# A recurrent attention layer and a two-matrix expert on one core: group 2 turned by a transposing DMA, and all steps put in another order

## The chip, the core and the metric

One NeuronCore of a Trainium2 chip. Its engines run side by side, each through its own list of instructions in order, and wait for one another by semaphores: TensorE (PE, matrix products into PSUM), VectorE (DVE), ScalarE (ACT), GpSimd (POOL) and SyncE (SP), whose list holds only DMA issues. The metric is the device time of one execution in microseconds. Three runs of the kernel before gave 175.01, 175.27 and 175.44 us, median 175.27.

## The reference

Two layers follow one another. The first is a linear recurrence for 4 batches, 8 heads, 768 steps and a head width of 48; the second is a product with `w_in`, a smooth gate, and a product with `w_out`.

```python
for t in range(S):
    kt, vt, rt = k[:, :, t], v[:, :, t], r[:, :, t]
    cur = np.einsum('bhd,bhe->bhde', u[None] * kt, vt)
    y[:, :, t] = np.einsum('bhd,bhde->bhe', rt, state + cur)
    state = w[None, :, :, None] * state + np.einsum('bhd,bhe->bhde', kt, vt)
...
x = y.transpose(0, 2, 1, 3).reshape(B * S, H * D)      # 3072 x 384
h = x @ w_in                                           # 384 x 2048
g = np.where(h >= 1, h, np.where(h <= -1, 0, (h + 1) ** 2 / 4))
return g @ w_out                                       # 2048 x 384
```

## The kernel before

**Tiling.** The 768 steps are cut into 6 chunks of 128, the 4 batches into 2 pairs. A *group* g (0 to 11) is one chunk of one pair, so group g has chunk g // 2. A *unit* n (0 to 23) is one batch of a group, n = 2g + j. Inside a chunk the recurrence is computed as matrix products; `states` carry it from chunk to chunk.

**Steps.** The program is a list of small steps, each written as one token in the string `ORDER`. The loop at the end of the kernel walks through it, and each token issues the instructions of one step. A token reads `name.arguments@engine:buffers`; `@A`, `@D` and `@P` choose ACT, DVE or POOL where a step can run on several. The order of the tokens is therefore the order of every engine's list, and nothing is moved afterwards. A `~9` behind a token puts 9 matmuls on zeros ahead of it, and `warm.18` is 18 such matmuls; they compute nothing.

The steps of group g or unit n:

- `load.K.g`, `load.R.g`, `loadV.g` fetch inputs on SP's queue (384 KB each; groups 0 and 1 come in halves `g.0`, `g.1`). `V.g` casts V to bfloat16; the float32 tile that `loadV` fills may be fetched anew only after the cast that reads it.
- `Ks.g`, `Rs.g` scale K and R by powers of the decay (for groups 0 and 1 by the table `tab` in PSUM). `KU.g`, `RKU.g`, `usum.g` and `V2.g` make the diagonal term: K times u, times R, summed over a head, times V.
- `T.n` turns Ks and Rs on PE for groups 0 to 2 and `TT.n` copies the result out; from group 3 on `KRT.K.g` and `KRT.R.g` do it with a transposing DMA on SP's queue.
- `A.n` multiplies the turned tiles, `AT.n` masks the product (DVE in one instruction, or ACT copies and POOL masks).
- `Sp.n`, `Tm.n`, `decay.n`, `sbf.n` move the state on by one chunk. `Y.n` adds state and chunk terms in PSUM, `y.n` adds V2.
- y has to be turned before the second layer. For groups below `X_DMA` this is `X.n` (three transposes on PE) and `xT.n` (a copy out of PSUM by ACT); above it `y` writes into a tile `yy` for both units, and one `xT` of the group is a transposing DMA on SP's queue.
- `w_in.0`, `w_in.1` and `w_out.0` to `w_out.3` load the weights on POOL's queue, in POOL's list.
- `mm1.g.q.j` multiplies a group by quarter q of `w_in` (j = -1 for both units at once), `relu`, `square` (ACT) and `gate` (DVE) make the gated tile, `mm2.g.j.q` multiplies it by a quarter of `w_out`. `o` copies the result out and `out` stores it. The PSUM tiles `h0` to `h2` are shared by T, A and mm1.

**Lines.** `Ks` and `Rs` are L325, `KU` L335, `RKU` L342, `usum` L353 and L355, `V2` L365 and L367, `KRT` L396, `A` L404, `AT` L410 to L419, `Sp` L430, `Tm` L466 to L474, `X` L491, `xT` L501, `mm1` L516, `mm2` L544.

```python
X_DMA = 3
...
if g < X_DMA:
    copy(e, tiles["xT", g][:, j], tiles.pop(("X", n)))
else:
    nc.sync.dma_start_transpose(
        out=tiles["xT", g].rearrange("p u k t -> p (u k) t"), in_=tiles["yy", g].rearrange("p u d -> p (u d)")
    )
```

Of the kernel before, what the change touches and what calls it, by code (L numbers as in the profile page):

```python
# [33 lines left out]
warm.18 load.K.0.0:0 load.R.0.0:0 load.K.0.1 load.R.0.1 load.K.1.0:1 load.R.1.0:1 bcu:0 u_bc@D KU.0.0@P:0 RKU.0.0@P:0  # L34
lw loadV.0.0:0 bcw:1 load.K.1.1 KU.0.1@D loadV.0.1 wcol:0 Wdn_p:0 Ks.0.0@D:0 Wup_p load.R.1.1 Rs.0.0@D:0 wCm
KU.1.0@P:1 loadV.1.0:1 Ks.1.0@D:1 warm.4.h.2 T.0:1 load.K.2.0:2 Wdn RKU.1.0@P:1 Rs.1.0@D:1 Rs.0.1@D V.0.0@A:0
RKU.0.1@P T.2:2~9 TT.0@A:0 usum.0.0@D:0 Ks.1.1@D Ks.0.1@D KU.1.1@P Wup Sp.0:0 TT.2@D:1 A.0:1 V.0.1@A load.R.2.0:2
# [5 lines left out]
relu.0.0:0 X.3:0 Tm.5@D:0 mm1.0.1.0:1 AT.4.0:1 xT.3@A decay.5 square.0.0:0 usum.2.0@D:0 Sp.4:1 mm1.0.1.1 w_out.0 Y.4:0
relu.0.1:1 mm1.1.1.-1:0 gate.0.0:0 square.0.1:1 Tm.4@D:1 mm1.0.2.-1:2 relu.1.1:0 Y.5:1 square.1.1:0 V2.2.0@P:0 w_out.1
y.4:1 gate.0.1:1 w_out.2 X.4:0 w_out.3 mm1.0.3.-1:1 xT.4@A:2 gate.1.1:2 relu.0.2:1 Sp.3:0 y.5:2 mm1.1.0.-1:0
square.0.2:1 Tm.3@D KU.3.0@P:1 decay.4 gate.0.2:3 relu.0.3:0 relu.1.0:1 mm2.0.0.0:1 mm2.0.1.0:0 Ks.3.0@P:0 RKU.3.0@D:1
square.1.0:0 KRT.K.3:0 mm1.1.3.-1:2 mm2.0.1.1 Rs.3.0@P:0 mm2.0.0.1 square.0.3:1 gate.1.0:4 mm2.0.1.2 gate.0.3:5
relu.1.3:1 loadV.3.0:1 mm2.0.0.2 mm1.1.2.-1:0 square.1.3:0 usum.3.0@D:1 mm2.0.0.3 relu.1.2:0 KRT.R.3:0 mm2.0.1.3
o.0.0@D:0 square.1.2:1 mm2.1.0.0:1 o.0.1@D gate.1.3:6 load.K.4.0:1 X.5:0 mm2.1.0.1 load.R.4.0:1 xT.5@A V.3.0@A:3
mm1.2.3.-1:1 gate.1.2:7 sbf.3@A V2.3.0@P:1 Sp.7:0 A.7:2 loadV.4.0:0 relu.2.3:1 Tm.7@D:0 A.6:0 mm2.1.0.2 AT.6.0:2  # L50
sbf.2@A square.2.3:0 Ks.4.0@P:2 sbf.4@A Sp.6:0 mm2.1.0.3 load.K.5.0:2 Tm.6@D:1 mm1.2.0.-1:0 o.1.0@A:1 AT.7.0:3 decay.6
Y.6:0 Y.7:1 relu.2.0:0 KRT.K.4:1 y.6:0 mm1.2.1.-1:2 KU.4.0@P:0 y.7 V.4.0@A:4 gate.2.3:8 xT.6:1 RKU.4.0@P:0
square.2.0:1 mm2.1.1.0:0 Sp.8:1 mm2.1.1.1 load.R.5.0:2 Tm.8@D:1 relu.2.1:1 load.K.6.0:0 mm1.2.2.-1:1 gate.2.0:9
Ks.5.0@P:1 mm2.1.1.2 square.2.1:0 mm2.2.0.0:1 mm2.1.1.3 decay.7 Rs.4.0@P:1 mm1.3.0.-1:0 gate.2.1:0 relu.2.2:0
square.2.2:1 KRT.K.5:0 mm2.2.0.1 o.1.1@D sbf.5@A relu.3.0:1 mm1.3.1.-1:2 gate.2.2:1 out.1 KU.5.0@P:1 square.3.0:0
Rs.5.0@P:2 mm2.2.0.2 relu.3.1:0 gate.3.0:3 mm1.3.2.-1:1 KRT.R.4:1 square.3.1:1 loadV.5.0:1 load.R.6.0:0 usum.4.0@D:0
mm2.2.0.3 mm2.2.1.0:0 KU.6.0@P:0 relu.3.2:1 gate.3.1:5 mm1.3.3.-1:0 square.3.2:0 loadV.6.0:0 gate.3.2:4 mm2.2.1.1
V2.4.0@P:0 sbf.6@A o.2.0@A:1 A.9:2 sbf.7@A relu.3.3:0 A.8:1 AT.9.0:1 mm2.2.1.2 KRT.R.5:0 square.3.3:1 mm2.3.0.0:1
AT.8.0:0 out.0 decay.8 mm2.2.1.3 load.K.7.0:1 mm2.3.0.1 o.2.1@A gate.3.3:2 V.6.0@A:0 V.5.0@A:2 Y.8:0 Ks.6.0@P:0
mm2.3.0.2 y.8:1 Y.9:0 mm2.3.0.3 y.9 RKU.5.0@P:1 A.11:2 xT.8:0 o.3.0@A:0 A.10:1 usum.5.0@D:1 AT.11.0:2 mm2.3.1.0:0  # L60
Sp.10:1 KRT.K.6:1 mm2.3.1.1 Rs.6.0@P:0 RKU.6.0@P:0 Tm.10@D:0 mm2.3.1.2 load.R.7.0:1 Sp.9:1 mm2.3.1.3 Tm.9@D:1
V2.5.0@P:1 mm1.4.0.-1:0 AT.10.0:3 o.3.1@A sbf.8@A decay.9 decay.10 KRT.R.6:1 usum.6.0@D:0 relu.4.0:1 Sp.11:1 Y.10:0
mm1.4.1.-1:2 square.4.0:0 Tm.11@D:1 y.10:0 V2.6.0@P:0 Ks.7.0@P:2 Y.11:1 mm1.4.2.-1:1 loadV.7.0:0 out.2 relu.4.1:0
gate.4.0:7 y.11 A.12:0 xT.10:2 square.4.1:1 AT.12.0:0 mm2.4.0.0:0 Sp.12:1 relu.4.2:1 KU.7.0@P:1 square.4.2:0
gate.4.1:6 load.K.8.0:2 mm1.4.3.-1:0 V.7.0@A:1 KRT.K.7:0 gate.4.2:9 load.R.8.0:2 A.13:2 Rs.7.0@P:1 mm2.4.0.1 out.3
Tm.12@D:0 mm1.5.0.-1:1 AT.13.0:1 RKU.7.0@P:1 relu.4.3:0 square.4.3:1 relu.5.0:1 gate.4.3:0 loadV.8.0:1 square.5.0:0
sbf.9@A decay.12 mm2.4.0.2 Y.12:1 mm1.5.2.-1:2 usum.7.0@D:1 mm2.4.0.3 Ks.8.0@P:1 y.12:1 mm1.5.1.-1:0 gate.5.0:1
o.4.0@A:1 Y.13:1 KRT.R.7:0 relu.5.2:0 V2.7.0@P:1 KRT.K.8:1 Sp.13:0 square.5.2:1 mm1.5.3.-1:1 y.13 Tm.13@D:0 decay.11
relu.5.1:1 xT.12:1 gate.5.2:8 mm2.4.1.0:1 KU.8.0@P:0 Sp.14:0 square.5.1:0 mm2.4.1.1 load.K.9.0:0 Tm.14@D:1 mm2.4.1.2
relu.5.3:0 sbf.10@A gate.5.1:3 mm2.5.0.0:0 Rs.8.0@P:2 A.15:2 square.5.3:1 A.14:0 AT.15.0:3 mm2.4.1.3 mm2.5.0.1  # L70
V.8.0@A:3 KRT.R.8:1 decay.13 RKU.8.0@P:0 AT.14.0:2 mm1.6.0.-1:2 o.4.1@A load.R.9.0:0 gate.5.3:5 Y.14:1 mm2.5.0.2
Ks.9.0@P:0 y.14:0 relu.6.0:1 mm1.6.1.-1:0 square.6.0:0 usum.8.0@D:0 gate.6.0:4 loadV.9.0:0 load.K.10.0:1 mm2.5.0.3
mm2.5.1.0:1 sbf.11@A sbf.12@A A.17:1 relu.6.1:0 o.5.0@D:0 KU.9.0@P:1 A.16:2 mm2.5.1.1 AT.17.0:0 V2.8.0@P:0 decay.14
Rs.9.0@P:0 square.6.1:1 sbf.13@A Y.15:0 mm2.5.1.2 mm1.6.2.-1:1 y.15 V.9.0@A:4 AT.16.0:1 xT.14:0 KRT.K.9:0 Sp.15:0
RKU.9.0@P:1 gate.6.1:2 mm2.5.1.3 load.R.10.0:1 mm1.6.3.-1:2 relu.6.2:1 square.6.2:0 relu.6.3:0 o.5.1@D Tm.15@D:0
mm2.6.0.0:1 gate.6.2:7 out.5 Y.16:0 mm1.7.1.-1:0 decay.15 square.6.3:1 y.16:1 KRT.R.9:0 Ks.10.0@P:2 Sp.17:0 Tm.17@D:1
gate.6.3:6 load.K.11.0:2 mm2.6.0.1 relu.7.1:1 mm1.7.0.-1:1 KU.10.0@P:0 square.7.1:0 sbf.15@A mm2.6.0.2 Sp.16:0
relu.7.0:0 KRT.K.10:1 loadV.10.0:1 gate.7.1:9 mm1.7.2.-1:2 Rs.10.0@P:1 Tm.16@D:0 mm2.6.0.3 square.7.0:1 o.6.0@A:0
sbf.14@A usum.9.0@D:1 Y.17:0 mm1.7.3.-1:0 decay.16 y.17 relu.7.2:1 gate.7.0:0 RKU.10.0@P:0 mm2.6.1.0:1 square.7.2:0
Sp.18:0 KRT.R.10:1 mm2.6.1.1 Tm.18@D:0 sbf.16@A decay.17 A.18:1 gate.7.2:1 out.4 mm2.7.0.0:0 relu.7.3:0 xT.16:2  # L80
KU.11.0@P:1 mm2.6.1.2 square.7.3:1 AT.18.0:2 V2.9.0@P:1 mm2.7.0.1 load.R.11.0:2 loadV.11.0:0 Ks.11.0@P:1 mm2.6.1.3
gate.7.3:3 mm2.7.0.2 A.21:2 sbf.17@A V.10.0@A:2 o.6.1@A A.19:1 AT.21.0:3 A.20:0 mm2.7.0.3 AT.19.0:1 out.6 Y.18:1
o.7.0@A:1 y.18:0 mm1.8.0.-1:2 relu.8.0:1 KRT.K.11:0 AT.20.0:0 Y.19:0 mm1.8.1.-1:1 y.19 mm2.7.1.0:1 square.8.0:0
usum.10.0@D:0 xT.18:1 Sp.19:0 mm2.7.1.1 Tm.19@D:1 relu.8.1:0 mm1.8.2.-1:0 gate.8.0:8 square.8.1:1 mm2.7.1.2 decay.19
V2.10.0@P:0 relu.8.2:1 V.11.0@A:0 gate.8.1:5 Y.20:0 mm2.7.1.3 mm1.8.3.-1:2 decay.18 square.8.2:0 y.20:1 RKU.11.0@P:1
relu.8.3:0 o.7.1@D gate.8.2:4 square.8.3:1 out.7 mm1.9.0.-1:1 Rs.11.0@P:2 mm2.8.0.0:0 relu.9.0:1 gate.8.3:2 Y.21:1
mm2.8.0.1 KRT.R.11:0 usum.11.0@D:1 square.9.0:0 mm1.9.1.-1:0 y.21 xT.20:0 mm1.9.3.-1:2 relu.9.1:0 gate.9.0:7
square.9.1:1 mm2.8.0.2 mm2.8.1.0:1 relu.9.3:1 gate.9.1:6 mm1.9.2.-1:1 square.9.3:0 mm2.8.1.1 mm2.8.0.3 mm2.8.1.2
relu.9.2:0 V2.11.0@P:1 gate.9.3:0 o.8.0@D:0 A.22:0 sbf.19@A square.9.2:1 A.23:2 AT.22.0:2 mm2.8.1.3 mm2.9.0.0:0
AT.23.0:1 mm1.10.3.-1:0 o.8.1@A sbf.18@A Y.22:1 mm2.9.0.1 relu.10.3:1 mm1.10.2.-1:2 y.22:0 gate.9.2:9 Y.23:1  # L90
relu.10.2:0 mm1.10.0.-1:1 y.23 xT.22:2 square.10.2:0 mm2.9.0.2 relu.10.0:0 mm2.9.1.0:1 gate.10.2:1 mm2.9.0.3
square.10.0:1 mm2.9.1.1 mm1.10.1.-1:2 square.10.3:0 out.8 gate.10.0:3 mm2.9.1.2 gate.10.3:8 relu.10.1:0 mm1.11.0.-1:1
# [535 lines left out]
```

## Time and profile before

| what | value |
|---|---|
| median of three runs | 175.27 us |
| the profiled execution: its time, its span | 175.03 us, 173.3 us |
| first matmul of the second layer (mm1.0.0) | 21.46 us after the span's start |
| end of the last matmul | 169.8 us |
| TensorE clock granted | 1.00 in every slice |
| packets of the SP queue | 103888, 25.27 MB, 75.2% of 16 DMA engines' span |

A row of the profile gives a start and a duration in us, the engine, the line, the operation, the tiles it writes and reads, and in brackets the idle time of the engine before it with what ended it. Line numbers in the profile of before are those of the listing above. The span is shorter than the time of the execution by 1.7 us, which lie outside the program's instructions.

### The profile page before, as it was taken

How to read it: one execution, taken by the hardware profiler on the slowest of the kernel's cores; microseconds unless marked ns; L12 is line 12 of the kernel's file. 1: busy time of each engine (PE TensorE's matmuls, PEld its weight loads, DVE VectorE, ACT ScalarE, POOL GpSimd, SP SyncE). 2: the span in 40 equal slices, each digit the busy share in tenths (PEclk: the TensorE clock that was granted, in tenths of full speed). 3: DMA queues.
4: the chain of work that ended last, by engine and by line, in shares of the span. 5: the costliest groups of instructions: out<-in, count | busy, mean ns of one | idle time of the engine just before them, and what ended most of it. 6: DMA issues, size and time to landing. Idle time of an engine off the chain costs nothing.

```text
span 173.3 us, 4141 instructions
## 1 busy us (share of the span) xinstructions
PE 163.5 (94%) x1674; PEld 123.7 (71%) x1674; DVE 134.8 (78%) x168; ACT 134.9 (78%) x194; POOL 118.1 (68%) x96
## 2 busy tenths in 40 slices
...
GB/s 110 224 223 198 223 185 232 201 173 206 240 175 200 246 159 255 154 186 238 183 235 182 210 213 155 232 229 253 229 77 95 106 2 4 128 8 95 0 91 91
...
## 3 DMA queue, kind: packets, MB, share of 16 engines
q1 hardware_dynamic: 103888, 25.27, 75.2%
q0 software_dynamic: 2912, 3.15, 11.3%
...
## 4 chain that ended last, share of the span: by engine, by line
PE 71%; DMA 10%; DVE 9%; ACT 5%; issue 2%; POOL 1%; SPq 1%; DVEq 0%; POOLq 0%
PE hp L516 33%; PE op L544 30%; DMA VF<-in_v_dram 5%; DVE AT L419 3%; DMA xT<-yy 3%; PE A L404 3%; DVE RKU L342 2%; DMA K<-in_k_dram 2%; DVE gt L534 2%; PE Y L444 2%; PE Y L439 2%; PE Sp L430 1%; ACT V L210 1%; ACT RKU L353 1%; POOL V L367 1%
## 5 line engine op out<-in xcount | busy, mean ns | idle before, releaser
L516 PE MATMUL hp<-xT,w_in_sb 128*128 128x256 bf16 (+1 forms) x600 | 70.8, 268 | 2.7 <-DVE gt L534 1.0
L544 PE MATMUL op<-w_out_sb,gt 128*128 128x384 bf16 x384 | 71.7, 326 | 0.0
L534 DVE SCALAR_TENSOR_TENSOR gt<-sq,hp 128x1024 bf16<-128x1024 f32 x48 | 57.9, 1216 | 14.6 <-ACT sq L529 14.3
L516 PEld LDWEIGHTS <-w_in_sb 128*128 128x128 bf16 x600 | 55.8, 98 | 12.8 <-issue 2.9
L524 ACT ACTIVATE pt<-hp 128x1024 f32<-128x1024 f32 x48 | 48.6, 1017 | 13.5 <-PE hp L516 13.3
L529 ACT ACTIVATE sq<-pt 128x1024 f32<-128x1024 f32 x48 | 50.4, 1057 | 3.0 <-DVE gt L534 1.8
L544 PEld LDWEIGHTS <-gt 128*128 128x128 bf16 x384 | 35.6, 98 | 19.7 <-issue 0.2
L419 DVE TENSOR_TENSOR AT<-A,umask 128x1024 bf16<-128x1024 f32 x22 | 26.5, 1218 | 1.8 <-PE A L404 1.5
L367 POOL TENSOR_TENSOR V<-V,diag 128x768 f32<-128x768 bf16 (+1 forms) x12 | 16.5, 1375 | 9.1 <-ACT V L210 7.1
L335 POOL TENSOR_TENSOR KU<-K,u_bc 128x768 f32<-128x768 f32 (+1 forms) x13 | 21.3, 1640 | 1.9 <-DVE u_bc L210 1.8
L342 POOL TENSOR_TENSOR RKU<-R,KU 128x768 f32<-128x768 f32 (+1 forms) x13 | 20.7, 1595 | 0.3
L325 POOL TENSOR_TENSOR Ks<-Wdn,K 128x768 bf16<-128x768 f32 x10 | 18.3, 1828 | 2.1 <-PE Y L444 1.7
L479 POOL TENSOR_TENSOR state<-Tm,wCm 128x384 f32<-128x384 f32 x16 | 16.1, 1008 | 5.1 <-DVE Tm L466 5.1
L325 POOL TENSOR_TENSOR Rs<-Wup,R 128x768 bf16<-128x768 f32 x10 | 18.3, 1830 | 0.0
L458 DVE TENSOR_TENSOR yy<-Y,V 128x384 bf16<-128x384 f32 x18 | 9.9, 553 | 5.0 <-PE Y L444 3.5
L210 ACT CAST V<-VF 128x768 bf16<-128x768 f32 (+1 forms) x14 | 10.2, 736 | 2.7 <-DMA VF<-in_v_dram 2.7
L466 DVE TENSOR_TENSOR Tm<-Sp,state 128x384 f32<-128x384 f32 x16 | 8.9, 553 | 4.3 <-PE Sp L430 3.4
L444 PE MATMUL Y<-V,AT 128*128 128x48 bf16 x192 | 11.2, 184 | 1.1 <-POOL AT L414 0.7
L210 ACT COPY oo<-op 128x384 f32<-128x384 f32 x13 | 6.2, 475 | 7.6 <-PE op L544 7.5
L444 PEld LDWEIGHTS <-AT 128*128 128x128 bf16 x192 | 9.5, 96 | 2.7 <-POOL AT L414 1.0
L355 DVE TENSOR_REDUCE diag<-RKU 128x16 f32<-128x768 f32 (+1 forms) x13 | 11.0, 850 | 0.0
L210 ACT CAST state_bf<-state 128x384 bf16<-128x384 f32 x20 | 10.0, 504 | 0.0
...
## 6 DMA issues: line engine op xcount, KB each, us to landing
out_dram<-oo SPq DMA_DIRECT2D x11, 384.0 KB, 3.3
K<-in_k_dram SPq DMA_DIRECT2D x10, 384.0 KB, 4.6
R<-in_r_dram SPq DMA_DIRECT2D x10, 384.0 KB, 4.1
VF<-in_v_dram SPq DMA_DIRECT2D x10, 384.0 KB, 5.7
...
w_out_sb<-in_moe_w_out_dram POOLq DMA_DIRECT2D x4, 384.0 KB, 7.4
...
```

The source lines that it names most:

```text
L210: nc.scalar.copy(out, in_) if e == "A" else engines[e].tensor_copy(out, in_)
L325: engines[e].tensor_mul(of_unit(dst, j0, j1)[:, :, :, :D], rep(tab, j1 - j0), of_unit(tiles[what, g], j0, j1))
L335: engines[e].tensor_mul(of_unit(tiles["KU", g], j0, j1), of_unit(tiles["K", g], j0, j1), rep(u_bc, j1 - j0))
L342: engines[e].tensor_mul(of_unit(tiles["RKU", g], j0, j1), of_unit(tiles["R", g], j0, j1), of_unit(tiles["KU", g], j0, j1))
L367: engines[e].tensor_mul(tiles["V2", g][:, hs, :], tiles["V", g][:, hs, :], tiles["diag", g][:, hs].unsqueeze(2).to_broadcast([P, hs.stop - ...
L419: nc.vector.tensor_mul(t.rearrange("p i n t -> p (i n) t"), tiles.pop(("A", n)).rearrange("p i n t -> p (i n) t"), umask.unsqueeze(1).to_b ...
L444: nc.tensor.matmul(t[:, 2 * p + i, :], tiles["AT", n][:, i, p, :], tiles["V", g][:, j * H + 2 * p + i, :], start=(c == 0), stop=True, skip ...
L516: nc.tensor.matmul(hp[:, f, cols], w_in_sb[:, i, n0 : n0 + P], tiles["xT", g][:, units, i, :], start=(i == 0), stop=(i == nK - 1), skip_gr ...
L524: nc.scalar.activation(tiles["pt", g, q], tiles["hp", g, q], AF.Relu, bias=0.5, scale=0.5)
L529: nc.scalar.activation(tiles["sq", g, q], tiles.pop(("pt", g, q)), AF.Square, bias=0.0)
L534: nc.vector.scalar_tensor_tensor(out=gt, in0=tiles.pop(("sq", g, q)), scalar=1.0, in1=tiles.pop(("hp", g, q)), op0=ALU.min, op1=ALU.max)
L544: nc.tensor.matmul(tiles["op", g, j], tiles["gt", g, q][:, f, j * P : (j + 1) * P], w_out_sb[:, n, :], start=(n == 0), stop=(n == nF - 1),)
```

## The change

`X_DMA` goes from 3 to 2: y of group 2 (units 4 and 5) goes into `yy`, and one transposing DMA on SP's queue takes the place of `X.4`, `X.5` (six PE transposes) and the two copies `xT.4`, `xT.5` on ACT. The string `ORDER` is another one from end to end. Within it some steps change engine: `RKU.3` goes from DVE to POOL; `KU.0.0`, `RKU.0.0` go from POOL to DVE and `KU.0.1` from DVE to POOL; `TT.0` goes from ACT to DVE; `Tm.0` and `Tm.2` go from DVE to ACT, where each is eight small multiplies; `usum.1.0` from ACT to DVE; the four half steps V2 of groups 0 and 1 trade places between ACT and POOL; and of the copies `o` seven go from DVE to ACT (0.1, 1.1, 5.1, 8.0, 10.0, 10.1, 11.0) and two from ACT to DVE (4.0, 7.0). Matmuls on zeros are 54 in place of 68. The constants `W_OUT = 4` and `FUSE = ()` and the branch on `FUSE` are new; with these values they issue the same instructions as before.

```diff
 TABLES = 2
 W_IN = 2
+W_OUT = 4
+FUSE = ()
 NSPLIT = 2
 SPLIT = 2
 T_DMA = 3
 T_TAG = "h"
-X_DMA = 3
+X_DMA = 2
...
-    n = slice(i * FG, (i + 1) * FG)
+    n = slice(i * nF // W_OUT, (i + 1) * nF // W_OUT)
...
-    nc.vector.tensor_add(t, flat(tiles.pop(("Y", n))), flat(tiles["V2", g][:, j * H : (j + 1) * H, :]))
+    Yn = tiles.pop(("Y", n))
+    if g in FUSE:
...
+    else:
+        nc.vector.tensor_add(t, flat(Yn), flat(tiles["V2", g][:, j * H : (j + 1) * H, :]))
...
-T.4:0 TT.5@D:0 Y.1:0 w_in.1 load.K.3.0:0 xT.0@A:1 sbf.1@A usum.1.1@D A.5:1 mm1.0.0.0:2 KU.2.0@P:0 y.1:2 TT.4@D:1
+V2.0.1@P A.4:0~2 TT.5@D:3 load.K.3.0:0 V2.1.0@P:1 Tm.1@D y.2:1 w_in.1 Y.3:0 A.5:1 sbf.0@A V2.1.1@A Y.1:1 sbf.1@A
```

The prediction speaks of three places in the order. The first is ACT's list from the cast of V of unit 2 to the first relu. Before (L353 is usum, the rows V_340 and V_333 are V2, L210 is any copy or cast):

```order
L210 CAST V<-VF 128x384
L353 ACTIVATE RKU,diag<-RKU 128x48 x8
L365 ACTIVATE V_340<-V,diag 128x48 x8
L210 CAST state_bf<-state 128x384
L410 CAST AT<-A 128x1024
L365 ACTIVATE V_333<-V,diag 128x48 x8
L210 COPY xT<-X 128x384 x2
L210 CAST state_bf<-state 128x384
L210 CAST V<-VF 128x384
L210 COPY xT<-X 128x384
L210 CAST V<-VF 128x768
L524 ACTIVATE pt<-hp 128x1024
```

And in the changed kernel, over the same stretch (L482 is Tm, once for unit 0 and once for unit 2; line numbers are about 10 higher at the end of the file):

```order
L212 CAST V<-VF 128x384
L482 ACTIVATE state<-Sp,wc_col 48x48 x16
L412 CAST AT<-A 128x1024
L212 COPY xT<-X 128x384
L212 CAST V<-VF 128x384 x2
L212 CAST state_bf<-state 128x384
L367 ACTIVATE V_454<-V,diag 128x48 x8
L212 CAST state_bf<-state 128x384
L212 COPY xT<-X 128x384
L212 CAST V<-VF 128x768
L212 COPY xT<-X 128x384 x2
L534 ACTIVATE pt<-hp 128x1024
```

The casts of the second halves of V (the row x2) now stand behind Tm and AT.1; before, that of unit 0 stood ahead of everything shown. Two copies xT stand behind the cast of V of group 2.

The second place is POOL's list from the second half of `w_in` to the scaling of group 3. Before:

```order
L288 DMA w_in_sb<-in_moe_w_in_dram 128x3x1024
L335 TENSOR_TENSOR KU<-K,u_bc 128x768
L367 TENSOR_TENSOR V_340<-V,diag 128x384
L342 TENSOR_TENSOR RKU<-R,KU 128x768
L479 TENSOR_TENSOR state<-Tm,wCm 128x384
L292 DMA w_out_sb<-in_moe_w_out_dram 128x4x384
L367 TENSOR_TENSOR V_670<-V,diag 128x768
L292 DMA w_out_sb<-in_moe_w_out_dram 128x4x384 x3
L335 TENSOR_TENSOR KU<-K,u_bc 128x768
L479 TENSOR_TENSOR state<-Tm,wCm 128x384
L325 TENSOR_TENSOR Ks<-Wdn,K 128x16x48
L325 TENSOR_TENSOR Rs<-Wup,R 128x16x48
```

In the changed kernel:

```order
L290 DMA w_in_sb<-in_moe_w_in_dram 128x3x1024
L294 DMA w_out_sb<-in_moe_w_out_dram 128x4x384
L337 TENSOR_TENSOR KU<-K,u_bc 128x768
L344 TENSOR_TENSOR RKU<-R,KU 128x768
L369 TENSOR_TENSOR V_618<-V,diag 128x768
L294 DMA w_out_sb<-in_moe_w_out_dram 128x4x384
L489 TENSOR_TENSOR state<-Tm,wCm 128x384
L294 DMA w_out_sb<-in_moe_w_out_dram 128x4x384 x2
L337 TENSOR_TENSOR KU<-K,u_bc 128x768
L327 TENSOR_TENSOR Ks<-Wdn,K 128x16x48
L344 TENSOR_TENSOR RKU<-R,KU 128x768
L327 TENSOR_TENSOR Rs<-Wup,R 128x16x48
```

`w_out.0` is issued right behind `w_in.1`; `w_out.1` stands behind V2 of group 2, and RKU of group 3 has come in between Ks and Rs of group 3.

The third place is SP's list around the new transposing DMA. Before, from the load of V of group 2:

```order
L302 DMA VF<-in_v_dram 128x16x48
L302 DMA K<-in_k_dram 128x16x48
L302 DMA R<-in_r_dram 128x16x48
L396 DMA_TRANSPOSE KT<-Ks 128x8x128
L302 DMA VF<-in_v_dram 128x16x48
L396 DMA_TRANSPOSE RT<-Rs 128x8x128
L302 DMA K<-in_k_dram 128x16x48
```

In the changed kernel:

```order
L304 DMA VF<-in_v_dram 128x16x48
L304 DMA K<-in_k_dram 128x16x48
L304 DMA R<-in_r_dram 128x16x48
L398 DMA_TRANSPOSE KT<-Ks 128x8x128
L511 DMA_TRANSPOSE xT<-yy 128x6x128
L304 DMA K<-in_k_dram 128x16x48
L398 DMA_TRANSPOSE RT<-Rs 128x8x128
L304 DMA VF<-in_v_dram 128x16x48
```

The new xT stands directly behind the KT of group 3, and V of group 3 is fetched behind RT of that group.

More of the change, by code (lines that the diff above doesn't have):

```diff
@@ L28 @@
 T_TAG = "h"
-X_DMA = 3
+X_DMA = 2
 ORDER = """
[L34 to L37, printed above, removed]
@@ L43 @@
[L43 to L47, printed above, removed]
@@ L48 @@
[L48 to L92, printed above, removed]
@@ L93 @@
[L93 to L97 removed]
+warm.18 load.K.0.0:0 bcu:0 lw load.R.0.0:0 u_bc@D KU.0.0@D:0 RKU.0.0@D:0 usum.0.0@D:0 loadV.0.0:0 load.K.0.1
```

76 lines of the change are left out of this document (67 added, 9 removed).

## The prediction

> **What bounds the kernel now.** First the page's busy times and its chain of waits, then the table by stretches.
>
> ```profile
> PE 163.5 (94%) x1674; PEld 123.7 (71%) x1674; DVE 134.8 (78%) x168; ACT 134.9 (78%) x194; POOL 118.1 (68%) x96
> PE 71%; DMA 10%; DVE 9%; ACT 5%; issue 2%; POOL 1%; SPq 1%; DVEq 0%; POOLq 0%
> 45.00:70.00 25.00, 24.93 (x254) 18.31 (x253) 19.44 (x23) 21.61 (x28) 24.92 (x16) 1.00 1.20 210
> 70.00:90.00 20.00, 18.63 (x219) 14.62 (x219) 16.55 (x20) 14.37 (x18) 19.44 (x15) 1.00 1.02 197
> 90.00:170.00 80.00, 79.78 (x764) 59.12 (x762) 59.48 (x66) 63.22 (x75) 39.12 (x26) 1.00 0.61 128
> ```
>
> The columns behind a stretch are its length and the busy time of PE, weight loads, DVE, ACT and POOL. PE is the bound: 71% of the chain. From 90 us on it lacks 0.22 us of 80, so a new order has nothing to win there and can only lose. From 45 to 90 us it is idle for 0.07 + 1.37 = 1.44 us, and POOL is busy for 44.4 of 45. What is left is the start, where the chain leaves PE. PE's "busy" there contains matmuls on zeros, so I read the chain in order of time instead (start, duration):
>
> ```profile
> 9.69 0.40 ACT V L210
> 10.09 0.91 ACT TT L210
> ...
> 11.88 0.91 ACT AT L410
> 12.80 0.43 ACT V L210
> ...
> 15.10 8.50 DMA VF<-in_v_dram
> ...
> 23.63 0.84 ACT V L210
> ...
> 26.56 0.87 DVE diag L355
> ...
> 27.58 1.48 POOL V L367
> ...
> 34.32 4.15 DVE RKU L342
> ...
> 46.91 0.17 PE Sp L430 x4
> ...
> 49.05 0.04 PE Y L439
> ...
> 49.79 1.31 PE hp L516 x12
> ...
> 57.14 0.65 PE op L544 x4
> ...
> 70.02 4.57 DMA xT<-yy
> ```
>
> ACT's list paces the start; then the load of V of group 2, issued at 15.1, holds ACT until 23.6. PE's prices come from here too: a quarter of mm1 1.31 us, of mm2 0.65, one Sp 0.17, and two Y from 49.05 to 49.79, so 0.37 for one. Single steps, from the timeline (start, duration, in brackets the idle time ahead and what ended it):
>
> ```profile
> 14.94 0.84 POOL L367 TENSOR_TENSOR V<-V,diag 128x384 f32<-128x384 bf16 x1
> 14.94 1.90 ACT L365 ACTIVATE V<-V,diag 128x48 f32<-128x48 bf16 x8
> 19.86 0.84 ACT L210 COPY xT<-X 128x384 bf16<-128x384 bf16 x2
> 20.31 0.80 POOL L288 DMA_DIRECT2D w_in_sb<-in_moe_w_in_dram  x1
> 24.36 1.02 ACT L524 ACTIVATE pt<-hp 128x1024 f32<-128x1024 f32 x1
> 27.34 1.21 DVE L534 SCALAR_TENSOR_TENSOR gt<-sq,hp 128x1024 bf16<-128x1024 f32 x1
> 28.61 1.47 PE L516 MATMUL hp<-xT,w_in_sb 128*128 128x256 bf16 x12 [0.17 <-DVE gt L534]
> 35.80 1.84 POOL L325 TENSOR_TENSOR Rs<-Wup,R 128x768 bf16<-128x768 f32 x1
> 39.69 1.06 ACT L529 ACTIVATE sq<-pt 128x1024 f32<-128x1024 f32 x1 [1.77 <-DVE gt L534]
> 45.54 0.62 PE L404 MATMUL A<-RT,KT 48*128 48x128 bf16 x16
> ```
>
> The 28.61 row is mm1.0.2, the first step that needs a PSUM tile back from a gate and the second half of `w_in`; the 45.54 row is A of group 3. Between these two I compare the orders. Landing times of DMAs from their issue, of the tiles VF and w_in_sb (both up to 50 us) and xT, and two lines of the DMA view:
>
> ```profile
> DMA to landing us min/median/max: 3.8/5.0/9.6
> ...
> DMA to landing us min/median/max: 8.0/8.3/8.5
> ...
> DMA to landing us min/median/max: 2.7/2.8/4.6
> ...
> w_out_sb<-in_moe_w_out_dram POOLq DMA_DIRECT2D x4, 384.0 KB, 7.4
> ...
> RT<-Rs SPq DMA_TRANSPOSE x9, 4.6
> ```
>
> **The change, part by part.** *PE's own work.* X.4 and X.5 go: 0.34 us, three transposes priced like the four matmuls of Sp. The work between mm1.0.2 and A of group 3 is counted from each order. Before: six quarters of mm1, ten of mm2, one Y, two X, two Sp: 7.86 + 6.50 + 0.37 + 0.34 + 0.34 = 15.41 us. That took 45.54 - 28.61 = 16.93, so 1.5 us were stalls. Now: the same mm1 and mm2 and one Sp, 14.53 us; Y.5 stands ahead of the stretch, X.4 and X.5 are gone, and one Sp comes behind it (+0.17).
>
> *DVE's new first steps.* KU.0.0, RKU.0.0 and usum.0.0 now stand ahead of Ks.0.0, with which ACT's second table, T.0 and A.0 begin.
>
> ```profile
> 5.68 0.99 POOL L335 TENSOR_TENSOR KU<-K,u_bc 128x384 f32<-128x384 f32 x1 [1.83 <-DVE u_bc L210]
> 5.74 1.35 DVE L335 TENSOR_TENSOR KU<-K,u_bc 128x384 f32<-128x384 f32 x1
> ...
> 7.01 0.55 DVE L325 TENSOR_TENSOR Ks<-tab,K 128x384 bf16<-128x384 f32 x1
> ...
> 34.03 1.85 POOL L325 TENSOR_TENSOR Ks<-Wdn,K 128x768 bf16<-128x768 f32 x1
> ```
>
> DVE's KU ended at 7.09, 0.42 us behind POOL's. RKU of group 3, started at 34.32, ended at 38.47, 0.83 us behind POOL's Rs (35.80 + 1.84): it stood through two POOL products. So half a group of such a product costs DVE 0.42 alone. POOL's KU.0.1 has to wait for its load, now one place later, so I let DVE go first: Ks.0.0 starts at 5.74 + 0.42 + 0.42 + 0.55 (usum, priced like Ks) = 7.1 to 7.2, 0.2 late. If KU.0.1 gets in first, RKU.0.0 waits 1.0 more. [...]
>
> *ACT up to the first relu.* Ahead of the copy AT.0 the list loses V.0.0, V.0.1 (0.40 each) and TT.0 (0.91) and gains V2.0.0 (1.90): +0.2. With DVE's 0.2, AT.0 starts at 12.3 instead of 11.88. Behind it come V.1.0 0.43, Tm.0 and Tm.2, AT.1 0.91, xT.0 0.42 and V.0.1 0.40. A Tm on ACT is eight small multiplies and has no row; the nearest is the ACT row of eight at 1.90, its lower bound a single instruction, 0.40, its upper 2.1 if PSUM is slower. I take 1.90 twice. V.0.1 ends at 12.3 + 0.91 + 0.43 + 3.80 + 0.91 + 0.42 + 0.40 = 19.2. Only then may SP fetch V of group 2 into the tile that V.0.1 read: 4.1 us later than at 15.1, with K and R of group 3 queued behind it on SP. Between the median 5.0 and the maximum 9.6 I take 5.7, a little over the median since both halves of `w_in` are under way: it lands at 24.9. The cast (0.84) and two copies xT (0.84) now stand ahead of relu.0.0: 26.6 against 24.36. Relu, square and gate take 1.02 + 1.06 + 1.21 and some 0.2 between them. **mm1.0.2 starts at 30.1 instead of 28.61: +1.5.** `w_in.1` comes close but does not decide: AT.0's mask on POOL is 0.4 late and one more half of V2 (0.84) stands ahead of it, so it is issued at 20.31 + 1.2 = 21.5 and lands at 29.8. `w_in.0`, behind AT.0's mask now, is covered by ACT's delay.
>
> *From there to A of group 3.* ACT gives a gate every 2.08 us. mm1.1.2 needs the second at 32.2, some 0.6 after PE could start it. `w_out.1` stands on POOL behind KU.2, RKU.2 (1.84 each, like Rs), and V2.2 (1.48), which waits for usum.2 (0.87): from `w_out.0`'s end at 23.1 that is 29.2, landing at 36.6 by 7.4, where PE wants it at 36.1. With a further 0.2 at a gate the stalls are 1.3 to 1.4, as before: RKU.3, which kept DVE from its gates for 4.15 us and ACT idle for 1.77, does so no longer, and the late start gives that back. Ks.3 ends on POOL at 36.4, with decay and two `w_out` issues ahead of it; KT leaves SP then and the new xT behind it at 37.8. It lands 2.7 to 4.6 later, at 42.4 at worst; mm1.2.3 stands at 43.4, so **the new DMA is hidden** by 1 us, and what it comes later than that it costs. RKU.3 moves Rs.3 on POOL from 37.64 to 40.1; RT, 4.6 behind, lands at 44.7, under A at 46.0. V of group 3 is fetched only behind RT, near 41.4: landing (5.0), cast (0.84), V2 (1.48), y (0.55) and transpose (4.6) end at 53.9, and mm1 of group 3 starts 9.5 us of PE work behind A, at 55.5: covered by 1.6 us. Together: +1.5 - (15.41 - 14.53) - 0.1 + 0.17 = **+0.7**. Bounds: V of group 2 lands in 3.8, so `w_in.1` holds mm1.0.2 at 29.8, and no stall is left: 0.7 - 0.3 - 1.4 = -1.0. V lands in 8.5, as that load did before: 0.7 + 2.8 = +3.5.
>
> *From 45 to 90 us.* PE's one wait for a transposing DMA was that of group 4:
>
> ```profile
> PE hp L516 <- DMA xT<-yy: 1.0, 1, 1.0
> ```
>
> Between that group's last Y and its first mm1 stand 4.15 us of PE work before and 3.67 now (counted like the work above): with a landing of 4.57 again the wait grows by 0.5. Group 8 has 3.99 (8.17 before): a wait of 0 to 1.1. The shortest stretch from an mm1 to its mm2 falls from 3.81 to 3.22 us, under the 3.5 of relu, square and gate. If xT lands in 2.8, no such wait is left. I take +0.4, with bounds of -1.4 (all idle time gone) and +1.6. The copies `o` that change engine hide under the next mm2.
>
> **Sum.** The profiled execution took 175.03 us (its span of 173.3 and 1.7 around it), 0.24 below the median of 175.27. 175.03 + 0.7 + 0.4 = **176.1 us**.
>
> **Rivals.** *Faster (0.28).* The loads are less crowded: while SP waits for V.0.1, K and R of group 2 drain, V of group 2 lands in 3.8 and `w_out.1`, issued apart from the others, in 5. Nothing stalls up to A of group 3, -1.0, and xT of group 4 at 2.8 takes its 1.0 too: 173.0; with one of the two, 174.0. It decides if relu.0.0 starts before 25. For it: a queue that stands still leaves room. Against: the POOL chain to `w_out.1` is made of its own durations.
>
> *Much slower (0.17).* V of group 2 shares the DMA engines with `w_in` and takes 8.5 as before: relu.0.0 at 29.4, +2.8, giving 178.9. It decides from a landing past 27. For it: that very load took 8.50 in the chain. Against: then three loads were in the queue ahead of it.
>
> *No change (0.13).* The new DMA is hidden, and what the start loses (0.7) shorter transposes give back from 45 to 90 us: 175.0.
>
> **How the numbers follow.** The forecast, a small loss, has 0.42, its own range 175.3 to 177.3. About 0.3% (0.5 us) is what a measurement of this kernel can tell from no change. Faster is the first rival and a sliver of the forecast: 0.30. Same is the third: 0.13. Slower is the rest: 0.57. The range for 8 in 10 reaches from 173.7, past half of the first rival, to 179.0, past the second's figure.
>
> **What would show it.** Right: the cast of V of group 2 ends past 25, relu.0.0 is near 26.6, mm1.0.2 near 30.1, A of group 3 near 46.0; PE does not wait for xT of group 2 and waits 1 to 1.5 us for that of group 4. Wrong: that cast before 24.5, a Tm on ACT far from 1.9 us, RKU.0.0 on DVE over 0.6, or new PE waits past 90 us, which I have not priced.

## The result, and the profile after

| | before | after |
|---|---|---|
| median of three runs | 175.27 us | 178.36 us (178.07 to 178.37) |
| ratio after to before | | 1.0173, 95% interval 1.0147 to 1.0198 |
| the profiled execution: its time, its span | 175.03 us, 173.3 us | 178.07 us, 176.4 us |

The changed kernel is slower by 3.1 us. Some executions of one and the same kernel take longer than its others (one of b_x2 178.84 us, its nine others 174.61 to 176.35); the ratios of this document leave out those over 1.5% above the fastest. The forecast of 176.1 was added up from the profiled execution of before, so it is to be held against the profiled 178.07: 2.0 us have to be found. First the same views as before: the busy times and the chain of the changed kernel's page.

```profile
PE 164.8 (93%) x1654; PEld 125.4 (71%) x1654; DVE 128.8 (73%) x163; ACT 139.0 (79%) x196; POOL 119.1 (68%) x96
PE 55%; DMA 17%; ACT 9%; POOL 8%; issue 4%; DVE 3%; SPq 1%; ACTq 0%; POOLq 0%
```

PE's share of the chain fell from 71% to 55%, and DMA's rose from 10% to 17%: more of the end is set by transfers. DVE lost 6 us of work and ACT gained 4. The table by stretches of the changed kernel (length; busy time of PE, weight loads, DVE, ACT, POOL; granted clock; DMA share; GB/s) tells where:

```profile
15.00:25.00 10.00, 6.97 (x112) 6.17 (x109) 6.97 (x11) 9.70 (x30) 7.90 (x8) 0.83 0.88 154
45.00:70.00 25.00, 24.58 (x259) 18.33 (x258) 20.66 (x23) 21.13 (x28) 23.18 (x15) 1.00 1.11 216
70.00:90.00 20.00, 19.70 (x218) 14.95 (x216) 16.75 (x20) 16.95 (x22) 18.98 (x14) 1.00 1.10 205
100.00:110.00 10.00, 8.73 (x92) 6.31 (x91) 7.95 (x11) 6.12 (x8) 7.47 (x6) 1.00 1.02 205
120.00:130.00 10.00, 9.78 (x94) 7.30 (x91) 8.26 (x9) 9.37 (x13) 10.00 (x8) 1.00 1.08 205
```

And two of the same stretches in the kernel before:

```profile
15.00:25.00 10.00, 8.15 (x147) 6.77 (x148) 7.96 (x14) 8.38 (x26) 9.98 (x8) 1.00 1.12 195
...
100.00:110.00 10.00, 10.00 (x113) 7.65 (x112) 8.59 (x12) 8.57 (x10) 10.00 (x7) 1.00 0.94 207
```

PE lost 1.2 us of busy time between 15 and 25, and 1.3 between 100 and 110, where it had not been idle at all. From 45 to 90 it is now idle for 0.42 + 0.30 = 0.72 us, against 1.44 before.

Because the orders differ, one start time against another says little. So I add to the start of a group's first mm1 the PE work that still stands behind it in that order, at the prediction's prices. This is where PE would end if it never waited again; the difference after minus before is the loss so far.

| first mm1 of group | started before | started after | loss so far |
|---|---|---|---|
| 0 | 21.46 | 25.31 | +3.0 |
| 2 | 43.97 | 44.57 | +1.9 |
| 6 | 95.86 | 95.63 | +1.1 |
| 7 | 107.60 | 109.33 | +2.6 |
| 9 | 131.32 | 134.43 | +3.1 |
| 11 | 153.32 | 155.77 | +3.1 |

So the start lost 1.9, the middle gave 0.8 back, and 2.0 went late: 1.5 at one place near 104 us and 0.5 between groups 7 and 9.

**The start.** The timeline of the changed kernel (start, duration, in brackets the idle time ahead and what ended it):

```profile
14.98 4.93 ACT L482 ACTIVATE state<-Sp,wc_col 48x48 f32<-48x48 f32 x16 [1.16 <-PE Sp L432]
19.96 0.48 PE L501 MATMUL X<-ident,y 128*128 128x128 bf16 x3 [2.12 <-ACT state L482]
21.02 1.09 POOL L416 TENSOR_SCALAR_AFFINE_SELECT AT<-AT 128x1024 bf16<-128x1024 bf16 x1 [2.08 <-ACT AT L412]
21.35 0.93 ACT L212 CAST V<-VF 128x384 bf16<-128x384 f32 x2
21.89 0.37 SPq L304 DMA_DIRECT2D VF<-in_v_dram  x1
22.08 1.61 POOL L369 TENSOR_TENSOR V<-V,diag 128x384 f32<-128x384 bf16 x2
23.64 0.80 POOL L290 DMA_DIRECT2D w_in_sb<-in_moe_w_in_dram  x1
...
26.87 0.83 ACT L212 CAST V<-VF 128x768 bf16<-128x768 f32 x1
28.35 1.05 ACT L534 ACTIVATE pt<-hp 128x1024 f32<-128x1024 f32 x1
32.43 1.48 PE L526 MATMUL hp<-xT,w_in_sb 128*128 128x256 bf16 x12 [0.56 <-DMA w_in_sb<-in_moe_w_in_dram]
47.33 0.62 PE L406 MATMUL A<-RT,KT 48*128 48x128 bf16 x16
```

The two Tm on ACT took 4.93 us, and ACT first waited 1.16 us for the Sp that they read. Three engines stand behind them. PE waited 2.12 us, because X.0 writes into the PSUM tile from which Tm reads. POOL waited 2.08 us for AT.1, and `w_in.1` stands behind that mask and two halves of V2: issued at 23.64, it ends the wait of mm1.0.2 at 32.43. SP could fetch V of group 2 only after V.0.1, the first of the two casts at 21.35: that load was issued at 21.89, and its cast ran at 26.87.

**Near 104 us.** SP's queue and ACT's list, both of the changed kernel:

```profile
96.56 1.22 SPq L583 DMA_DIRECT2D out_dram<-oo  x1
97.84 0.46 SPq L304 DMA_DIRECT2D VF<-in_v_dram  x1
...
103.45 0.83 ACT L212 CAST V<-VF 128x768 bf16<-128x768 f32 x1 [2.30 <-DMA VF<-in_v_dram]
104.33 0.33 PE L432 MATMUL Sp<-V,Ks 128*128 128x96 bf16 x4 [1.27 <-ACT V L212]
```

The load of V of group 8 is issued at 97.84, lands 5.6 us later, is cast, and Sp of group 8 has waited 1.27 us for it. In the new order 4.8 us of PE work lie between that load's place and this Sp; before there were 23.7. From group 3 on, the other groups of the new order have 8.5 to 12.2 up to their first Sp (group 3 has 5.8 up to a Y, which reads its V first). The shortest such stretch that the order of before has from group 3 on is that of group 4, 5.8, and PE did not wait there.

### The profile page after: what moved, and what is told of

It is laid out like the page before. It is cut to its first block, busy times and chain, and to the rows that moved or that the text cites. A ratio compares the mean times of both kernels' runs of the same rounds, so it can differ in the third digit from the quotient of the medians.

```text
span 176.4 us, 4091 instructions
## 1 busy us (share of the span) xinstructions
PE 164.8 (93%) x1654; PEld 125.4 (71%) x1654; DVE 128.8 (73%) x163; ACT 139.0 (79%) x196; POOL 119.1 (68%) x96
## 4 chain that ended last, share of the span: by engine, by line
PE 55%; DMA 17%; ACT 9%; POOL 8%; issue 4%; DVE 3%; SPq 1%; ACTq 0%; POOLq 0%
PE hp L526 24%; PE op L554 24%; DMA VF<-in_v_dram 5%; DMA w_in_sb<-in_moe_w_in_dram 5%; DMA xT<-yy 4%; ACT sq L539 3%; DMA R<-in_r_dram 2%; ACT pt L534 2%; POOL Rs L327 2%; PE Y L441 1%; PE Y L446 1%; PE A L406 1%; POOL AT L416 1%; ACT state_bf L212 1%; DMA u_row<-in_u_dram 1%
## 5 line engine op out<-in xcount | busy, mean ns | idle before, releaser
L344 POOL TENSOR_TENSOR RKU<-R,KU 128x768 f32<-128x768 f32 (+1 forms) x13 | 21.3, 1639 | 0.4
L468 DVE TENSOR_TENSOR yy<-Y,V 128x384 bf16<-128x384 f32 x20 | 10.9, 554 | 5.3 <-POOL V L369 2.5
L357 DVE TENSOR_REDUCE diag<-RKU 128x16 f32<-128x768 f32 (+1 forms) x14 | 11.5, 830 | 0.5 <-POOL RKU L344 0.5
L212 ACT COPY oo<-op 128x384 f32<-128x384 f32 x17 | 7.9, 472 | 1.3 <-PE op L554 1.0
```

Of the source, the lines that this page charges most:

```text
L212: nc.scalar.copy(out, in_) if e == "A" else engines[e].tensor_copy(out, in_)
L344: engines[e].tensor_mul(of_unit(tiles["RKU", g], j0, j1), of_unit(tiles["R", g], j0, j1), of_unit(tiles["KU", g], j0, j1))
```

## The experiments

Twelve kernels were run. Each diff is by tokens of `ORDER` against the kernel that is named.

| run | kernel and edit | ratio to before | 95% interval |
|---|---|---|---|
| b_x2 | before, group 2's y by DMA alone | 1.0013 | 0.9987 to 1.0039 |
| b_tm_act | before, Tm.0 and Tm.2 on ACT | 1.0301 | 1.0267 to 1.0334 |
| a_tm_dve | changed, Tm.0 and Tm.2 on DVE | 1.0139 | 1.0096 to 1.0181 |
| a_win1 | changed, `w_in.1` earlier | 1.0357 | 1.0285 to 1.0428 |
| a_tm_wo | a_tm_dve, `w_out.1` earlier | 1.0107 | 1.0068 to 1.0146 |
| a_out4 | changed, store of group 4 behind load of V of group 8 | 1.0215 | 1.0181 to 1.0248 |
| a_v8 | changed, load of V of group 8 earlier | 1.0167 | 1.0127 to 1.0207 |
| a_oo | changed, third tile `oo` for o.5.0 | 1.0224 | 1.0195 to 1.0253 |
| a_v8_oo | changed, a_v8 and a_oo | 1.0214 | 1.0187 to 1.0241 |
| a_tm_v8_oo | changed, a_tm_dve, a_v8 and a_oo | 1.0148 | 1.0088 to 1.0208 |
| a_tm_wo_v8 | a_tm_wo and a_v8 | 1.0206 | 1.0141 to 1.0272 |
| a_tm_late | a_tm_v8_oo, xT of group 7 ahead of two loads | 1.0235 | 1.0163 to 1.0307 |

The changed kernel itself is at 1.0173. 0.01 of a ratio is 1.75 us.

### The parts alone, in the order of before

**b_x2.** The headline of the change without the new order:

```diff
-X_DMA = 3
+X_DMA = 2
-X.4:0 X.5:0 xT.4@A:2 xT.5@A
-y.5:2
+y.5 xT.4:2
```

> The kernel before with X_DMA = 2 alone: X.4, X.5 and their two ACT copies go, one transposing DMA is issued on SP behind y.5, the order is else that of before. Theory (the new DMA is hidden; the loss is all in the order): 0.2 to 0.6 us faster than before, 174.7 to 175.1. Rival (the transposing DMA in the crowded early queue delays KT or the loads of group 3): 175.8 to 177.

No change can be told: by the interval it lies between 0.2 us faster and 0.7 us slower, so the theory's gain is not there, and of the rival's loss its lower end at most. In the order of before, the transposing DMA in place of six transposes is not where the time went; that leaves the new order. The new order with `X_DMA` = 3 was not run; in the changed kernel PE waits neither for this DMA nor for the RT of group 3 behind it.

**b_tm_act.** The one move on which the start seemed to hang, put into the order of before:

```diff
-Tm.0@D
+Tm.0@A
-Tm.2@D
+Tm.2@A
```

> The kernel before with Tm.0 and Tm.2 on ACT, nothing else. Theory S: ACT's list gets 4.9 us longer ahead of the first relu, which starts 2 to 4 us behind 24.36; 1 to 2.5 us slower, 176.3 to 177.8. Rival (ACT has room at the start, as its waits for V of group 2 show): 175.1 to 175.7.

This alone costs 5.2 us, more than the whole change and twice the most that its theory gave. Its timeline:

```profile
13.04 2.45 ACT L472 ACTIVATE state<-Sp,wc_col 48x48 f32<-48x48 f32 x8
16.08 0.33 PE L430 MATMUL Sp<-V,Ks 128*128 128x96 bf16 x4 [2.09 <-ACT V L210]
20.06 2.46 ACT L472 ACTIVATE state<-Sp,wc_col 48x48 f32<-48x48 f32 x8
22.56 0.48 PE L444 MATMUL Y<-V,AT 128*128 128x48 bf16 x8 [3.82 <-ACT state L472]
```

One Tm takes 2.45 us, and PE waits 2.09 us behind the first (for the cast that follows it on ACT) and 3.82 behind the second. In this order usum and V2 stand on ACT between the two, which the new order has put elsewhere; so the 5.2 us are the price of the move in a list not made for it, and not a term of the change's sum.

**a_tm_dve.** The reverse, in the changed kernel:

```diff
-Tm.0@A
+Tm.0@D
-Tm.2@A
+Tm.2@D
```

> The changed kernel with Tm.0 and Tm.2 back on DVE, nothing else. Theory S (the two Tm on ACT, 4.93 us there, hold AT.1 and V.0.1 and through them the second half of w_in and V of group 2): AT.1's mask on POOL starts near 19.0 instead of 21.02, w_in.1 is issued near 21.6 instead of 23.64, mm1.0.2 starts near 30.3 instead of 32.43, and the time falls by 1.0 to 1.5 us, to 176.9 to 177.4. Rival (the place of w_in.1 on POOL, behind two halves of V2, or the colder TensorE clock sets the start): no more than 0.4 us, 178.0 to 178.4.

Rows of its timeline:

```profile
21.64 0.80 POOL L290 DMA_DIRECT2D w_in_sb<-in_moe_w_in_dram  x1
26.54 1.05 ACT L534 ACTIVATE pt<-hp 128x1024 f32<-128x1024 f32 x1
30.07 0.80 POOL L294 DMA_DIRECT2D w_out_sb<-in_moe_w_out_dram  x1
37.37 0.81 PE L554 MATMUL op<-w_out_sb,gt 128*128 128x384 bf16 x4 [1.27 <-DMA w_out_sb<-in_moe_w_out_dram]
```

The waits behind Tm are gone: first mm1 at 23.50 in place of 25.31, the first relu 1.81 us earlier. But PE then waits 1.27 us for `w_out.1`, and the first mm1 of group 2 starts at 44.31, 0.26 earlier than in the changed kernel. The ratio is lower by 0.0034 or 0.6 us, inside both intervals, less than the theory's 1.0 and more than the rival's 0.4. Of 1.8 us gained at 25 us, most is given back by 44.

### Two more repairs of the start

**a_win1** issues `w_in.1` ahead of POOL's first scaling of group 2; **a_tm_wo** is a_tm_dve with `w_out.1` right behind `w_out.0`.

```diff
-w_in.1
-Ks.2.0@P:2
+w_in.1 Ks.2.0@P:2
```

```diff
-w_out.1
-w_out.0
+w_out.0 w_out.1
```

> The changed kernel with the second half of w_in issued on POOL ahead of Ks of group 2 instead of behind two halves of V2, Tm still on ACT. Theory S (Tm on ACT is the cause, w_in.1 only the last link): PE's wait of 0.56 us for w_in.1 goes, the first matmul of the second layer stays near 25.3, and the time falls by 0 to 0.5 us, to 177.9 to 178.4. Rival (the place of w_in.1 is the cause of the late start): 1 us or more, 177.4 or less.

> The changed kernel with both Tm on DVE and, on POOL, w_out.1 directly behind w_out.0 instead of behind V2 of group 2. Theory (with Tm gone from ACT the next thing that ends last at the start is w_out.1, for which PE waited 1.27 us at 37.37): that wait goes and the time falls by a further 0.8 to 1.3 us against Tm on DVE alone (177.75), to 176.4 to 177.0. Rival (w_out.1 earlier takes the bandwidth of K and R of group 3, and KT, RT or xT come late instead): 177.5 to 178.2.

`w_in.1` early is 3 us worse than the changed kernel, which neither the theory nor the rival had. PE's longest waits in it:

```profile
PE Y L446 <- ACT V L212: 2.2, 1, 2.2
PE X L501 <- ACT state L482: 2.1, 1, 2.1
...
PE A L406 <- DMA RT<-Rs: 1.2, 2, 1.0
```

The wait for `w_in` is gone, but PE waits 2.2 us for the cast of the second half of V of group 1, whose load, issued at 13.31, landed some 12.3 us later (Y started at 26.16, behind a cast of 0.51), against 5.8 in the changed kernel, and A waits 1.0 us for an RT. With `w_in.1` earlier the loads of V come late in its place, so this run does not tell which of the two held the start. a_tm_wo has the lowest ratio of all edits of the changed kernel: 1.0107, 1.2 us under the changed kernel with intervals that just touch, but not to be told from a_tm_dve. Its ratio rests on two executions (177.48 and 177.78 us), and the profiled one took 180.57, so I read no amounts from it; PE waits there for `w_out` still, and, as the rival said, for RT of group 3.

### The place near 104 us

**a_out4** and **a_v8** try the load of V of group 8 from two sides: the store ahead of it goes behind it, or the load itself goes up, behind the load of K of group 9.

```diff
-out.4
-loadV.8.0:0
+loadV.8.0:0 out.4
```

```diff
-load.K.9.0:0
+load.K.9.0:0 loadV.8.0:0
-loadV.8.0:0
```

> The changed kernel with the store of group 4 moved on SP behind the load of V of group 8, nothing else. Theory L (the store waits for the copy of op on ACT until 96.6 and holds the load of V of group 8 behind it, for which PE waits 1.27 us at 104.33): that load is issued near 96.1 instead of 97.84, PE's wait goes, and the time falls by 1.0 to 1.6 us, to 176.8 to 177.4. Rival (the load is late because the DMA engines are crowded, or the wait only moves): 178.0 to 178.5.

> The changed kernel with the load of V of group 8 moved forward on SP, from behind the store of group 4 to directly behind the load of K of group 9, nothing else. Theory L2 (a lead too short: 4.8 us of PE work lie between that load and the Sp that needs it, 23.7 before, and landing 5.5 and cast 0.84 need 6.3): it is issued near 92.9 instead of 97.84, PE's wait of 1.27 us at 104.33 goes, and the time falls by 1.0 to 1.6 us, to 176.8 to 177.4. Rival (the DMA engines are so crowded there that another load or RT comes late in its place, as with the store moved): 178.0 to 178.6.

In a_out4, without the store ahead of it, the load was issued 0.57 us earlier, at 97.27, and Sp's wait grew from 1.27 to 1.78 us. In a_v8, with the load at 92.75, the cast ran at 100.61 without waiting, and Sp waited all the same. From the timeline of a_v8:

```profile
97.52 1.20 SPq L583 DMA_DIRECT2D out_dram<-oo  x1
...
103.41 0.56 DVE L212 COPY oo<-op 128x384 f32<-128x384 f32 x1 [1.54 <-DMA out_dram<-oo]
...
104.12 0.33 PE L432 MATMUL Sp<-V,Ks 128*128 128x96 bf16 x4 [1.29 <-DVE oo L212]
```

A second cause had been ending at the same moment. o.5.0 copies into the tile `oo` that the store of group 4 still reads, and Sp needs the PSUM tile that o.5.0 empties. The rows of a_out4 fit this: the store went from 96.56 to 98.61 there, the cast of V ended at 103.57 + 0.83 = 104.40, and Sp started only at 105.35. The next two kernels take this wait away, alone and together with the load's, by a third tile:

```diff
-o.5.0@D:1
+o.5.0@D:2
```

> The changed kernel with one number changed: o.5.0, the copy of unit 0 of group 5 out of PSUM, writes into a third tile oo in place of tile 1, so that it no longer waits for the store out.4. Theory (the loss of 1.3 to 1.5 us near 104 us has two causes that end together, the late load of V of group 8 and this store): the store's wait goes from DVE, but TensorE's Sp still waits about 1.3 us, for ACT's cast of that V; 178.2 to 178.4 us, no gain. Rival (the store alone sets the end): Sp's wait goes and the time falls to about 177.0.

> The changed kernel with both repairs of the place near 104 us: the load of V of group 8 moved one place ahead on the SP queue (behind the load of K of group 9) and o.5.0 in a third tile oo. Theory (two causes that end together): Sp's wait of 1.3 us is gone, and so about 177.0 us, 1.0 to 1.4 under the changed kernel. Rival (something third is late there too, the xT of group 6 or a gate, since every wait taken away before came back elsewhere): less than 0.5 us gained, 178.

a_oo did as its theory said: Sp still waited 1.26 us for the cast of V, and nothing was gained. In a_v8_oo Sp's wait was gone for the first time, but the rival held: PE then waited 0.53 us for xT of group 7 and 1.09 us at 124.8 for a copy `o` on ACT, and nothing was gained either. a_tm_v8_oo adds Tm on DVE, to see whether the two ends add up.

> The changed kernel with Tm.0 and Tm.2 back on DVE and both repairs of the place near 104 us. Theory (two places of loss, far apart in time, which add): what Tm alone gained (0.3 to 0.6 us) and what the late pair gains (1.0 to 1.4): 176.4 to 176.8 us, still over the 175.3 of before by the rest of the start and the 0.6 us lost between groups 8 and 9. Rival (an early gain is absorbed by later waits): as with the late pair alone, 177.0.

At 1.0148 it is not better than a_tm_dve alone. The place in its timeline:

```profile
101.28 0.55 DVE L468 TENSOR_TENSOR yy<-Y,V 128x384 bf16<-128x384 f32 x1
...
102.71 0.57 SPq L304 DMA_DIRECT2D K<-in_k_dram  x1
103.34 1.64 SPq L304 DMA_DIRECT2D R<-in_r_dram  x1
105.08 2.72 SPq L511 DMA_TRANSPOSE xT<-yy  x1
...
109.65 0.61 PE L526 MATMUL hp<-xT,w_in_sb 128*128 128x256 bf16 x4 [1.74 <-DMA xT<-yy]
```

A third thing ends there: in this run y of group 7 is ready at 101.83, but its transpose stands on SP behind the KT of group 9 and the loads of K and R of group 10. In the changed kernel this lateness was covered by Sp's wait. The last kernel puts these loads behind the transpose:

```diff
-load.K.10.0:1
-load.R.10.0:1
-xT.14:1
+xT.14:1 load.K.10.0:1 load.R.10.0:1
```

> The kernel of Tm and the late pair (a_tm_v8_oo) with one more move on the SP queue: the loads of K and R of group 10 go behind the transposing DMA xT of group 7, whose y was ready at 101.8 us there while the xT was issued at 105.1. Theory (a third thing ends at the same place, xT held up by the two loads ahead of it on SP's queue): TensorE's wait of 1.74 us for xT near 109 goes or falls under 0.5, and the time falls by 1.0 to 1.7 us, from 178.1 to between 176.4 and 177.1. Rival (the DMA engines themselves are full there, so what is moved ahead delays what falls behind): the xT wait goes, but K or R of group 10 or a later transpose becomes a wait, and less than 0.5 us is gained, 177.7 to 178.2. In no case under the 175.4 of before, since the start still loses about 1 to 2 us.

The rival held, and more than held. From the table by stretches and the timeline of a_tm_late:

```profile
100.00:110.00 10.00, 10.00 (x108) 1.00 1.08 197
110.00:120.00 10.00, 10.00 (x116) 1.00 1.11 196
120.00:130.00 10.00, 7.80 (x68) 1.00 1.14 216
...
122.73 0.83 ACT L212 CAST V<-VF 128x768 bf16<-128x768 f32 x1 [3.54 <-DMA VF<-in_v_dram]
...
126.67 0.20 PE L441 MATMUL Y<-state_bf,RT 128*128 128x96 bf16 x1 [1.08 <-ACT oo L212]
```

PE (here the only engine shown) no longer waits between 100 and 120. It waits 2.2 us between 120 and 130 instead: ACT stands 3.54 us before the cast of V of group 10, whose load is now late, and all that is behind it on ACT comes late with it. The times on that chip scattered more than elsewhere (before itself 175.50 to 177.56 among the runs compared), so no gain over a_tm_v8_oo is what can be said, and a loss is likely.

**a_tm_wo_v8** had put three edits together before the second cause was known:

> All three at once: Tm on DVE, w_out.1 behind w_out.0, V of group 8 forward. If the three losses are apart and add up: 178.36 - 0.6 - 1.0 - 1.3 = 175.4, within 0.5 of the kernel before. Rival (the losses hide one another, another wait takes their place): 176.3 or more.

It was no faster than the changed kernel: Sp waited 1.19 us for o.5.0, and between 39 and 76 us PE waited six times, 0.3 to 0.9 us each, for `w_out`, RT and xT. None of the twelve beats the kernel before.

## Why the prediction was right in sign and short in size

**The bound and "it can only lose".** Right, and the part that mattered most was left unpriced. From 90 us on PE had no idle time to win, and there the new order lost 2.0 us, the largest single gap between sum and result. I had computed the lead of a transpose there (group 8, "a wait of 0 to 1.1"), but not that of the loads of V: 4.8 us of PE work for a load, a cast and a Sp, against a landing of 5.0 and a cast of 0.84 that the prediction itself quotes, says that PE waits. Counting this lead over all groups would have shown it. New PE waits past 90 us stood among the prediction's own signs of being wrong, and they came.

**PE's own work.** mm1.0.2 to A of group 3 took 47.33 - 32.43 = 14.90 us, for 14.53 us of counted work. So the count holds, and the stalls there were 0.4, not 1.3 to 1.4: what was late had become late already before mm1.0.2.

**DVE's first steps.** Ks.0.0 was put at 7.1 to 7.2. The timeline of the changed kernel:

```profile
5.64 0.56 DVE L337 TENSOR_TENSOR KU<-K,u_bc 128x384 f32<-128x384 f32 x1
6.24 0.56 DVE L344 TENSOR_TENSOR RKU<-R,KU 128x384 f32<-128x384 f32 x1
...
7.30 0.55 DVE L327 TENSOR_TENSOR Ks<-tab,K 128x384 bf16<-128x384 f32 x1
```

It started at 7.30. Each product alone took 0.56 where I had drawn 0.42 from the two that shared time with POOL. DVE went first, as assumed (POOL's KU.0.1 started at 6.60), so the case in which KU.0.1 gets in first, at 1.0 us more, did not arise.

**ACT's list, the term that was mis-sized.** "I take 1.90 twice", bounds 0.40 to 2.1: it took 4.93 us for both, 2.45 each in b_tm_act, outside the upper bound, which no row had given. The row that I went by was of the same width, but not out of PSUM. The list was followed from its own durations only: Tm stood 1.16 us waiting for PE's Sp, at 14.98 in place of 13.6. So V.0.1 ended near 21.9 in place of 19.2, the first relu started at 28.35 in place of 26.6, and mm1.0.2 at 32.43 in place of 30.1. And the step "`w_in.1` comes close but does not decide" failed: it was issued at 23.64, not 21.5, since POOL's masks wait for ACT's copies, and Tm stands ahead of AT.1's. It decided by 0.5 us over the gate, which ended at 30.70 + 1.21 = 31.91. mm1.0.2 came 3.8 us later than before, not 1.5, and the missing stalls behind it took a good part of that back: the start lost 1.9 us instead of 0.7, inside its bounds of -1.0 and +3.5. That Tm is the cause of the waits at 18 to 24 us is shown by a_tm_dve, where they go. That it is the cause of 1.9 us in the end is not: taking it away brought 0.6 by the ratios, and 1.2 with `w_out.1` moved too.

**V of group 2.** Its landing needed no 8.5 us, which takes the ground from the second rival: it was issued at the end of SP's wait, 21.89, and cast at 26.87, so it took at most 5.0. That rival's 178.9 is near the result by luck, since its way was another.

**The new transposing DMA is hidden.** Right. xT of group 2 left SP at 41.01 in place of 37.8, and mm1.2.3 at 44.57 did not wait for it. b_x2 shows the same in the order of before: none of PE's waits of 0.2 us or more is for an xT there.

**From 45 to 90 us.** Wrong in sign. PE was to wait 0.5 us more for xT of group 4; in all it waited 0.38 for xT of group 3 and 0.27 for that of group 4, where 0.98 had been. The 0.4 that was added for shorter leads was -0.7 in idle time (0.72 against 1.44 us) and -0.8 in the table.

The sum with measured terms: 175.03 + 1.9 - 0.8 + 2.0 = 178.1, the profiled 178.07. Up to 90 us it comes to +1.1, the very figure of the forecast, but only because two errors of 1.2 us cancel; the 2.0 that the time is off by are the late stretch, which had no term.

**What stays open.** Why the gains do not add up. At least three things ended together near 104 us, and each one taken away uncovered the next. One reading fits the rows, but no run tests it. Stretches of the changed kernel (length, granted clock, DMA share, GB/s):

```profile
21.00:23.00 2.00, 0.54 0.11 21
23.00:25.00 2.00, 1.00 1.12 226
...
25.00:100.00 75.00, 1.00 1.13 208
100.00:130.00 30.00, 1.00 1.05 197
```

While SP stood behind V.0.1, its queue ran dry: 21 GB/s between 21 and 23 us. From 15 to 25 the transfers moved 154 GB/s against 195 before, 0.41 MB less in 10 us, and a load is 384 KB. From there to 130 us the DMA share is above 1 on the average, so a load that is missing would stay missing, and the load of V of group 8 would be late by it. By this the two losses would be one. The record speaks against it. From the table by stretches and the timeline of a_tm_dve:

```profile
21.00:23.00 2.00, 1.34 (x32) 1.01 (x34) 2.00 (x4) 2.00 (x9) 2.00 (x3) 1.00 0.95 190
...
97.53 0.46 SPq L304 DMA_DIRECT2D VF<-in_v_dram  x1
103.04 0.83 ACT L212 CAST V<-VF 128x768 bf16<-128x768 f32 x1 [2.37 <-DMA VF<-in_v_dram]
```

There SP does not stand behind Tm and the queue does not run dry, yet the load of V of group 8 is issued only 0.31 us earlier, and PE waits 1.33 us for it. Between 15 and 25 us its transfers still moved 170 GB/s, under the 195 of before, so a part of the reading is left open.
